# A sequence layer and an expert layer in one kernel: the same 1728 pieces issued in another written order, each PSUM tile in a written bank

## The chip, the cores and the metric

One core of one Trainium2 chip runs the whole kernel. The metric is the device time of one execution in microseconds. The kernel before has three timed runs (504.03, 503.99 and 502.99 us, median 503.99 us) and one profiled execution, from which all rows below come.

## The reference, cut to what matters

The input `u` has 2048 rows of 512 channels. Two layers follow each other, each behind a layer norm, each added to its input:

```python
# layer 1: a long convolution along the rows, one kernel for each channel
P = exp((A * dt)[:, :, None] * pos)            # 512 channels x 128 states x 2048 positions, complex
K = 2 * einsum("dn,dnl->dl", C, P).real        # the convolution kernel of each channel
h = u + irfft(rfft(ln(u), 4096) * rfft(K, 4096))[:2048] + ln(u) * D_skip

# layer 2: 32 heads pick one of 256 experts for each row
q  = einsum("nd,dhc->nhc", ln(h), w_q)         # 512 -> 32 heads x 256
s1 = q[..., :128] @ k1.T ; s2 = q[..., 128:] @ k2.T      # 16 + 16 scores a head
e  = 16 * argmax(s1) + argmax(s2)              # one expert a head and row
h2 = h + sum_over_heads( gelu(ln(h) . u[e]) * v[e] )
```

With one expert a head the softmax over the picked scores is one, so it leaves no work.

## The kernel before, in words

The kernel is one long list of **pieces**. A piece is a small Python function that emits the instructions of one step on one engine (one group of matmuls, one copy, one product, one load), and `Plan.add` registers it with its engine, an estimated cost, the pieces it depends on and the PSUM bank pool that it takes from or gives back to. There are 1728 pieces. `Plan.run` emits them in the order of a written tuple of numbers, `ORDER` (L34 to L115). Each engine executes its own instructions strictly in the order of emission, and semaphores that follow from the data make an engine wait for another. So the tuple alone sets what stands behind what on every engine, the DMA queue of SP included.

The stages, in the order in which they mostly run:

- **Weights `w`.** 32 pieces load parts of `w_q` (L822, 512 KB each on SP), multiply them on PE with the expert keys (`wps`, L828), copy on ACT (L832), turn on PE (L836), copy (L840) and store to DRAM (L844). The result is `w_q` folded with the keys. These pieces wait for nothing but their load and a buffer, and are strewn between all the others.
- **Norm of the input.** SP loads `x` in eight parts of 512 KB, DVE takes statistics (`st`, L232), PE sums them over the partitions (`mu`, L242, and `va`, L255), ACT and DVE make the mean and the reciprocal spread (`pc`, L262 and L264).
- **Tables.** For each of 32 tables GpSimd (POOL in the profile) makes phases (`pg`, L557) and magnitudes (`mg`, L588, and the tail L594), ACT the sine and cosine into PSUM (`t`, L644 to L647), DVE their products (`gf` and `mg`, L651 to L664). PE then folds a table into the convolution kernel (`kps`, L690, 64 matmuls); this last is called the fold below. `pg`, `mg` and `gf` have two buffers, so the magnitudes of table i+2 are not written before the fold of table i has read its own.
- **Transforms.** For four chunks of channels the normed input (`xs`: subtract the mean L505, multiply L508; first transform `s1u`, L471; copied by ACT to `yu`, L474; second `s2yu`, L488, into `U`) and the convolution kernel (`s1k`, `s2yk`) are transformed and multiplied (L732 to L743), and transformed back in two steps, the first into `T` (`ia`, L764, copied at L772 and L777, stored to DRAM at L789), the second in the next layer.
- **The expert layer**, for eight blocks of 256 rows: second inverse transform and sum with the input (`ib` L1036, `h` L1043), the norm (`mean` L1093, `hc` L1073, squares on POOL into `vs`, L1060 to L1062, `hhi`/`hlo` L1076 and L1080), the scores (`sc` L1150), the inner products with all experts (`xu` L1157), the picked expert (`mx`, `eq`, `kq`, POOL's `ks` L1192, `ei` L1199, `ix` L1202) and the weighted sum: turn the index (`ixt` L1242), copy it to all partitions (`bc` L1258, copied by ACT to `idxb` L1262), one-hot rows on DVE (`oh` L1280), count on PE (`cnt` L1290), turn the activations (`ta` L1227), multiply (`actT` L1299), split in a high and a low half (`whi` L1302, `wlo` L1305), the sum over experts (`o` L1324 and L1327), the sum with `h` (`ob` L1332) and the store. The last block does the weighted sum in two halves of 128 rows.

PSUM holds three pools: `psA` with 7 banks up to the end of the transforms (the eighth bank is `pc`), then `psC` with 2 tiles of two banks for the scores and `psD` with 4 banks. In the kernel before each pool has `bufs` equal to its bank count and one tag for all its tiles, so the framework hands out the banks in rotation: the next tile gets the bank of the tile that was taken 7 (or 4) before it, and its first instruction waits until that tile has been read, whether another bank is free or not.

Of the kernel before, what the change touches and what calls it, by code (L numbers as in the profile page):

```python
# [9 lines left out]
F32 = mybir.dt.float32  # L10
# [9 lines left out]
P = 128  # L20
# [7 lines left out]
def view(t, off, dims):  # L28
# [89 lines left out]
class Plan:  # L118
# [5 lines left out]
    def __init__(self, slots):  # L124
        self.group = None
        self.ops, self.wr, self.rd, self.users, self.prev = [], {}, {}, {}, {}
        self.slots = {k: [0.0] * n for k, n in slots.items()}

    def ring(self, name, prev):

        self.prev[name] = prev
# [1317 lines left out]
```

## Time and profile before

| | |
|---|---|
| median of three runs | 503.99 us (502.99 to 504.03) |
| profiled execution, span from first to last instruction | 503.2 us |
| mean share of the span: PE, DVE, POOL, ACT | 89%, 81%, 65%, 59% |
| PE waits in total | 54.2 us, 35.6 of them before 71 us, 5.7 after 490 us |

The profile is of one execution, its span is the time from its first to its last instruction, and it lies 0.8 us under the median of the runs (inside their spread of 1.0 us). PE is TensorE's matmuls, PEld its weight loads, DVE VectorE, ACT ScalarE, POOL GpSimd, SP SyncE, which here only starts DMAs. In a row of a timeline stand the start and the length in us, the engine, the line, the operation, the tile written, `<-`, the tiles read, and in brackets the idle time of the engine before it with what ended it.

### The profile page before, as it was taken

Reading aid. Unit: us, or ns where it says so; the run is one execution under the profiler, and the core shown is the slowest. Engines: PE = TensorE matmul, PEld = TensorE weight load, DVE = VectorE, ACT = ScalarE, POOL = GpSimd, SP = SyncE. Lnnn points to the kernel's source line nnn. Section 1 sums busy time; section 2 is a strip of 40 time slices with the busy share of each in tenths; the row PEclk is TensorE's granted clock in tenths of the full one; section 3 lists DMA queues with packets and bytes.
Section 4 is the critical chain, followed back from the end, with each engine's and each line's share of the span. In section 5 each row is a group of like instructions: output and inputs, shape, how many; then the busy total and the mean of one; then the engine's idle time right before and its main releaser. Section 6 shows DMA issues by size and latency. Waiting matters only on the chain.

```text
span 503.2 us, 16702 instructions
## 1 busy us (share of the span) xinstructions
PE 449.0 (89%) x7206; PEld 390.3 (78%) x7206; DVE 407.8 (81%) x708; ACT 298.3 (59%) x594; POOL 325.5 (65%) x344
## 2 busy tenths in 40 slices
PE   0266879999998999999998889999999999999985
PEld 0144568888997999889997787877878888787874
DVE  5998998899968998899745574888979686978984
ACT  4867799967987588967965362644043430416230
POOL 4989989999999999997824303572163516536130
PEclk9998799999999999999999899999999999999999
DMA  8959474234033300631017689310171311010012
GB/s 253 403 198 381 143 288 148 66 86 179 2 111 124 85 3 1 212 126 45 1 61 259 200 275 283 127 61 1 57 227 55 109 63 43 1 44 0 1 68 62
DMA packets 27362, 61.05 MB, mean 121 GB/s; under 512 B 7028, under 2 KB 14456, under 8 KB 26136
## 3 DMA queue, kind: packets, MB, share of 16 engines
q1 hardware_dynamic: 27136, 59.85, 34.9%
q8 instruction: 57, 0.93, 0.7%
q10 hardware_dynamic: 152, 0.13, 0.1%
q14 instruction: 17, 0.14, 0.1%
HBM read 46.08 MB, written 13.89 MB: 119 GB/s over the span
## 4 chain that ended last, share of the span: by engine, by line
PE 50%; DVE 22%; ACT 10%; POOL 10%; issue 4%; DMA 3%; SPq 1%; ACTq 0%; DVEq 0%; POOLq 0%
PE sc L1150 12%; PE ia L764 9%; DVE oh L1280 5%; PE s2yk L488 3%; PE xu L1157 3%; PE kps L690 3%; PE s2yu L488 3%; POOL pg L557 3%; PE s1u L471 3%; DVE st L232 2%; PE o L1327 2%; PE ib L1036 2%; PE cnt L1290 2%; ACT t L645 2%; POOL mg L594 2%
## 5 line engine op out<-in xcount | busy, mean ns | idle before, releaser
L557 POOL TENSOR_TENSOR pg<-PS 128x1024 int32<-128x1024 int32 x32 | 68.8, 2150 | 0.5
L588 POOL TENSOR_TENSOR mg<-TS 128x1024 f32<-128x1024 f32 x32 | 62.6, 1958 | 7.2 <-PE kps L690 4.5
L1280 DVE TENSOR_SCALAR oh<-idxb,ec_s 128x2048 bf16<-128x2048 bf16 (+1 forms) x72 | 50.3, 757 | 6.8 <-ACT idxb L1262 6.8
L764 PE MATMUL ia<-ca_s,U 128*128 128x128 f32 x256 | 50.6, 280 | 0.4 <-POOL U L743 0.4
L1060 POOL TENSOR_TENSOR vs<-hc 128x256 f32<-128x256 f32 x8 | 7.0, 872 | 62.6 <-ACT hc L1083 62.6
L1192 POOL TENSOR_TENSOR ks<-kq 128x512 f32<-128x512 bf16 x16 | 17.2, 1078 | 45.9 <-DVE kq L1186 44.8
L645 ACT ACTIVATE t<-t,halfpi 128x512 f32<-128x512 f32 x64 | 42.4, 662 | 2.1
L1150 PE MATMUL sc<-w_hi,hhi 128*128 128x480 f32 x128 | 42.4, 412 | 0.0
L644 ACT ACTIVATE t<-pg 128x512 f32<-128x512 int32 x64 | 38.9, 609 | 3.2 <-DVE gf L652 2.2
L764 PEld LDWEIGHTS ia<-ca_s,U 128*128 128x128 f32 x256 | 39.8, 196 | 0.6 <-POOL U L743 0.6
L647 ACT ACTIVATE t<-pg 128x512 f32<-128x512 int32 x64 | 38.2, 608 | 2.8 <-POOL pg L557 1.5
L764 PE MATMUL ia<-ca_s,yk 128*128 128x128 f32 x192 | 38.1, 280 | 0.4 <-DVE mg L664 0.4
L1150 PE MATMUL sc<-w_lo,hhi 128*128 128x480 f32 x128 | 38.4, 380 | 0.0
L1150 PE MATMUL sc<-w_hi,hlo 128*128 128x480 f32 x128 | 38.3, 380 | 0.0
L594 POOL TENSOR_TENSOR mg<-TS 128x512 f32<-128x512 f32 x32 | 37.4, 1170 | 0.4
L690 PE MATMUL kps<-mg 128*32 128x64 f32 x1024 | 34.0, 230 | 3.8 <-DVE mg L664 2.2
L488 PE MATMUL s2yk<-yk,c_s 128*128 128x128 f32 x256 | 34.7, 282 | 1.1 <-ACT yk L474 0.7
L471 PE MATMUL s1u<-c_s,xs 128*64 128x128 f32 x512 | 33.3, 277 | 2.5 <-DVE xs L508 1.6
L690 PE MATMUL kps<-gf 128*32 128x64 f32 x1024 | 33.7, 229 | 1.8 <-issue 1.8
L488 PEld LDWEIGHTS s2yk<-yk,c_s 128*128 128x128 f32 x256 | 30.6, 191 | 4.2 <-issue 1.4
L488 PE MATMUL s2yu<-yu,c_s 128*128 128x128 f32 x256 | 32.6, 279 | 0.3
L471 PEld LDWEIGHTS s1u<-c_s,xs 128*64 128x64 f32 x512 | 27.6, 137 | 5.4 <-DVE xs L508 1.7
(198 smaller groups left out, 1377.5 us busy)
## 6 DMA issues: line engine op xcount, KB each, us to landing
wq<-wq SPq DMA_DIRECT2D x25, 512.0 KB, 4.5
t_d<-T SPq DMA_DIRECT2D x24, 256.0 KB, 3.4
Tb<-t_d SPq DMA_DIRECT2D x8, 768.0 KB, 6.0
x<-xa SPq DMA_DIRECT2D x8, 512.0 KB, 5.6
xs<-xb SPq DMA_DIRECT2D x16, 256.0 KB, 5.3
xt<-xt SPq DMA_DIRECT2D x8, 512.0 KB, 4.8
out<-ob SPq DMA_DIRECT2D x7, 512.0 KB, 3.0
c_s<-wq SPq DMA_DIRECT2D x4, 512.0 KB, 8.3
```

What stands on the lines that cost most here:

```text
L471: T.matmul(ps[64 * k:64 * k + 64, g, :], lhs8(4 * n + g), c1_s[:, k], start=True, stop=True)
L488: T.matmul(ps[:, k, :], c2_s[:, kk, :], y[:, :, kk, :], start=True, stop=True)
L557: G.tensor_tensor(view(pg, 0, [[32, 2 * NC], [8, 4], [1, 8]]), view(t["PS"], 1024 + off, [[1, 2 * NC], [128, 4], [0, 8]]), view(t["PS"], 8 ...
L588: G.tensor_tensor(view(mg, 0, [[96, NC], [8, 8], [1, 8]]), view(ts, 512 + 8 * o, [[8, NC], [1, 8], [0, 8]]), view(ts, 8 * o, [[8, NC], [0, ...
L594: G.tensor_tensor(view(mg, 64, [[96, NC], [8, 4], [1, 8]]), view(ts, 1536 + o, [[1, NC], [64, 4], [0, 8]]), view(ts, 1024 + 8 * o, [[8, NC ...
L644: A.activation(p, pg[:, :, k], AF.Abs)
L645: A.activation(p, p, AF.Sin, scale=-SINSCALE, bias=halfpi)
L647: A.activation(p, pg[:, :, k], AF.Sin, scale=SINSCALE)
L690: T.matmul(kps[32 * q:32 * q + 32, 2 * g + h, :], m[:, d, 64:96], m[:, d, 0:64], start=(e == 0), stop=(e == 1))
L764: T.matmul(ps[:, g, :], t[:, 4 * n + g].rearrange("p a b -> p (a b)"), ca_s[:, s, :], start=(s == 0), stop=(s == 1))
L1150: T.matmul(ps[:, 512 * h:512 * h + 480], t[x_][:, q, ts], I[w_][:, q, 480 * h:480 * h + 480], start=(q == 0 and x_ == w_), stop=(q == 3 an ...
L1280: V.tensor_scalar(oh[:, :, 0:ln], t["idxb"][:, :, sl], S["ec"][:, 4 * e + j:4 * e + j + 1], None, op0=ALU.is_equal)
```

## The change

The change adds and removes no arithmetic. All 1728 pieces, their functions, costs and dependences stay, and so does the number of matmuls. Two things differ.

First, `ORDER` is another order of the same numbers. Second, a dictionary `SLOT` with one digit for every tile that a pool hands out (351 for `psA`, 16 for `psC`, 131 for `psD`) now names the bank. `Plan.run` reads the next digit ahead of each piece that takes a bank, and the tile is made with a tag of its own for each bank, in pools of `bufs=1`. The tile then waits for the tile that had this bank last, 1 to 33 tiles before it in `psA` and 1 to 10 in `psD`, and no longer always 7 or 4. The lines of the changed kernel lie 11 further down (L690 becomes L701).

```diff
 ORDER = (
-    16, 0, 2, 1, 17, 18, 4, 23, 80, 3, 5, 9, 7, 24, 65, 19, 26, 20, 180, 21, 22, 10, 34, 6, 183, 35, 36, 197, 29, 185,
...
+    17, 0, 2, 5, 16, 1, 4, 18, 23, 3, 65, 75, 91, 6, 19, 20, 24, 26, 22, 27, 21, 28, 25, 29, 34, 35, 80, 66, 36, 37,
...
+SLOT = {
+    "psC": "0110101010101010",
...
+}
@@ Plan.__init__
         self.slots = {k: [0.0] * n for k, n in slots.items()}
+        self.slot, self.picks = None, {k: iter(v) for k, v in SLOT.items()}
@@ Plan.run
             done.add(n)
+            for k in self.ops[n][5]:
+                self.slot = next(self.picks[k])
             self.ops[n][3]()
@@ the pools
-    psA = ab.enter_context(tc.tile_pool(name="psA", bufs=7, space=PSUM))
+    psA = ab.enter_context(tc.tile_pool(name="psA", bufs=1, space=PSUM))
-        I["psC"] = ctx.enter_context(tc.tile_pool(name="psC", bufs=2, space=PSUM, reuse_waits="tile"))
-        I["psD"] = ctx.enter_context(tc.tile_pool(name="psD", bufs=4, space=PSUM, reuse_waits="tile"))
+        I["psC"] = ctx.enter_context(tc.tile_pool(name="psC", bufs=1, space=PSUM, reuse_waits="tile"))
+        I["psD"] = ctx.enter_context(tc.tile_pool(name="psD", bufs=1, space=PSUM, reuse_waits="tile"))
@@ one of the places where a tile is made; the others are changed alike
-            d["m"] = psA.tile([P, 4, 128], F32, tag="s", name="mu")[:, 0, 0:64]
+            d["m"] = psA.tile([P, 4, 128], F32, tag=f"s{plan.slot}", name="mu")[:, 0, 0:64]
```

Three places show what the new tuple moves.

On DVE, at the end of the head, where the input's norm becomes known: `xs` are the four normed chunks (the first number is the chunk), `pc` holds the mean and the spread, `gf` and `mg` belong to a table. Before, the steps of chunk 2 and a table's products stand between the steps of chunk 0:

```order
L505 TENSOR_TENSOR xs_2_280<-xs_2_280,pc 128x512
L655 TENSOR_TENSOR gf_905<-mg_888,t_5_871 128x16x32
L264 RECIPROCAL pc<-pc 128x64
L505 TENSOR_TENSOR xs_0_629<-xs_0_629,pc 128x512
L508 TENSOR_TENSOR xs_0_629<-xs_0_629,pc 128x512
L651 SCALAR_TENSOR_TENSOR gf_905<-mg_888,t_5_863 128x16x32
L652 TENSOR_TENSOR gf_905<-mg_888,t_5_863 128x16x32
L508 TENSOR_TENSOR xs_2_280<-xs_2_280,pc 128x512
```

Now:

```order
L516 TENSOR_TENSOR xs_0_921<-xs_0_921,pc 128x512
L275 RECIPROCAL pc<-pc 128x64
L519 TENSOR_TENSOR xs_0_921<-xs_0_921,pc 128x512
L516 TENSOR_TENSOR xs_2_841<-xs_2_841,pc 128x512
L519 TENSOR_TENSOR xs_2_841<-xs_2_841,pc 128x512
L666 TENSOR_TENSOR gf_924<-mg_873,t_5_880 128x16x32
```

Chunk 0 is finished right behind the reciprocal and chunk 2 right behind it, and the table's products come after both. In the same stage SP's list is changed: the last two of the eight loads of `x` stood behind a store of `w_d` and ahead of three loads of `w_q`; now they stand behind two loads of `w_q` and that store. On PE the statistics' sum `mu` stood behind the first two `s1k` pieces and ahead of the next two; now all four, and one `wps` group, stand ahead of it.

On PE, between the folds of tables 16 and 17 (the first and the second half of `kps2_0`). Before, three `s1k` pieces of 8 matmul rows each stand between them:

```order
L690 MATMUL kps2_0_2287<-gf16_2202 32x64 x4
L471 MATMUL s1k1_2_0_2325<-c1_s_84,k1_2_2030 64x128 x8
L471 MATMUL s1k1_3_1_2341<-c1_s_84,k1_3_2255 64x128 x8
L471 MATMUL s1k1_3_0_2353<-c1_s_84,k1_3_2255 64x128 x8
L690 MATMUL kps2_0_2287<-mg17_2218 32x64 x4
```

Now:

```order
L701 MATMUL kps2_0_2315<-gf16_2243 32x64 x4
L499 MATMUL s2yk1_0_2348<-yk1_2098,c2_s_85 128x128 x4
L499 MATMUL s2yk1_2_2362<-yk1_2098,c2_s_85 128x128 x4
L482 MATMUL s1u2_2_0_2367<-c1_s_84,xs2_2_1788 64x128 x8
L482 MATMUL s1u2_3_0_2376<-c1_s_84,xs2_3_2281 64x128 x8
L482 MATMUL s1u2_1_1_2385<-c1_s_84,xs2_1_1574 64x128 x8
L499 MATMUL s2yk1_4_2401<-yk1_2098,c2_s_85 128x128 x4
L482 MATMUL s1u2_1_0_2410<-c1_s_84,xs2_1_1574 64x128 x8
L701 MATMUL kps2_0_2315<-mg17_2239 32x64 x4
```

Seven pieces stand between the folds in place of three: the three `s1k` have gone ahead of the fold of table 16, and three `s2yk` and four `s1u` have come in.

On PE, in the last block's second half, the turned index (`ixt_128`), its copies (`bc`) and the inner products (`xu_1`). Before, twelve matmuls of `xu_1` stand ahead of the first copy:

```order
L1242 MATMUL ixt_128_7078<-ident_b,ix_7060 32x128
L1157 MATMUL xu_1_7083<-u_hi,hhi_6640 128x256
...
L1157 MATMUL xu_1_7083<-u_hi,hlo_6642 128x256
L1258 LDWEIGHTS sel_s
L1258 MATMUL bc_0_128_7097<-ixT_6991,sel_s 128x128
```

Now:

```order
L1253 MATMUL ixt_128_7073<-ident_b,ix_7071 32x128
L1238 MATMUL ta_0_7076<-ident,act_7037 128x128 x2
L1269 LDWEIGHTS sel_s
L1269 MATMUL bc_0_128_7081<-ixT_6992,sel_s 128x128
...
L1269 MATMUL bc_4_128_7086<-ixT_6992,sel_s 128x128
...
L1168 MATMUL xu_1_7130<-u_hi,hhi_6630 128x256
```

Both groups of copies now stand ahead of `xu_1`, and the counts `cnt` of the first half stand between. On DVE the one-hot rows of the second half now precede the multiplication `actT` of the first half, which stood ahead of them.

More of the change, by code (lines that the diff above doesn't have):

```diff
@@ L216 @@
     al, cra, sgn = (pb[:, k] for k in range(3))
-    sg, r64, w0, dt, r = (psA.tile([P, 512], F32, tag="s", name=f"par{k}") for k in range(5))
+    sg, r64, w0, dt, r = (psA.tile([P, 512], F32, tag=f"s{k}", name=f"par{k}") for k in range(5))
     w2 = pb[:, 3]
@@ L252, in var @@
         def var():
-            d["v"] = psA.tile([P, 4, 128], F32, tag="s", name="va")[:, 0, 0:64]
+            d["v"] = psA.tile([P, 4, 128], F32, tag=f"s{plan.slot}", name="va")[:, 0, 0:64]
             for e in range(2):
@@ L456, in bank @@
     def bank(job, nm, at="ps"):
-        job[at] = psA.tile([P, 4, 128], F32, tag="s", name=nm)
+        job[at] = psA.tile([P, 4, 128], F32, tag=f"s{plan.slot}", name=nm)
         return job[at]
@@ L1030, in mm @@
                 if 0 in js:
-                    job["ps"] = I["psD"].tile([P, 4, 128], F32, tag="m", name=f"ib{b}_{a}")
+                    job["ps"] = I["psD"].tile([P, 4, 128], F32, tag=f"m{plan.slot}", name=f"ib{b}_{a}")
                 for j in js:
@@ L1103, in mm @@
         def mm():
-            job["ps"] = I["psD"].tile([P, 256], F32, tag="m", name=f"mean{b}")
+            job["ps"] = I["psD"].tile([P, 256], F32, tag=f"m{plan.slot}", name=f"mean{b}")
             T.matmul(job["ps"], S["ones"], t["hs"], start=True, stop=True)
@@ L1121, in mm @@
         def mm():
-            ps = job["ps"] = I["psD"].tile([P, 2], F32, tag="m", name=f"var{b}")
+            ps = job["ps"] = I["psD"].tile([P, 2], F32, tag=f"m{plan.slot}", name=f"var{b}")
             for k in range(2):
@@ L1145, in mm @@
             if q == 0:
-                job["ps"] = I["psC"].tile([P, 1024], F32, tag="s", name="sc" + nm)
+                job["ps"] = I["psC"].tile([P, 1024], F32, tag=f"c{plan.slot}", name="sc" + nm)
             ps = job["ps"]
@@ L1153, in mx_ @@
         def mx_():
-            ps = jx["ps"] = I["psD"].tile([P, 256], F32, tag="m", name="xu" + nm)
+            ps = jx["ps"] = I["psD"].tile([P, 256], F32, tag=f"m{plan.slot}", name="xu" + nm)
             for q in range(4):
@@ L1224, in mm @@
             def mm(k=k, job=job):
-                tp = job["ps"] = I["psD"].tile([P, 2, 128], F32, tag="m", name=f"ta{b}_{k}")
+                tp = job["ps"] = I["psD"].tile([P, 2, 128], F32, tag=f"m{plan.slot}", name=f"ta{b}_{k}")
                 for e in range(2):
@@ L1239, in mm @@
             def mm(job=job, ks_=ks_, lo=lo):
-                job["ps"] = tp = I["psD"].tile([32, 256], BF16, tag="m", name=f"ixt{b}_{lo}")
+                job["ps"] = tp = I["psD"].tile([32, 256], BF16, tag=f"m{plan.slot}", name=f"ixt{b}_{lo}")
                 for k in ks_:
@@ L1286, in mm @@
                     if e == 0:
-                        job["ps"] = I["psD"].tile([P, 2, 256], F32, tag="m", name=f"cnt{b}_{lo}")
+                        job["ps"] = I["psD"].tile([P, 2, 256], F32, tag=f"m{plan.slot}", name=f"cnt{b}_{lo}")
                     for hg in range(8):
```

8 lines of the change are left out of this document (5 added, 3 removed), and 161 rows, old and new, of the table ORDER.

## The prediction, made before the changed kernel was run

> **What bounds the kernel now.** I read the page first, for who is busy when. The second fence row is the busy time of each engine, the two below it are the busy share of PE and of POOL in 40 slices of 12.6 us, in tenths:
>
> ```profile
> span 503.2 us, 16702 instructions
> ...
> PE 449.0 (89%) x7206; PEld 390.3 (78%) x7206; DVE 407.8 (81%) x708; ACT 298.3 (59%) x594; POOL 325.5 (65%) x344
> ...
> PE   0266879999998999999998889999999999999985
> ...
> POOL 4989989999999999997824303572163516536130
> ```
>
> PE is at 9 nearly everywhere behind the sixth slice. So I cut the span at the places where that digit falls and asked for the busy time of each engine in each stretch (length, then PE, PE's weight loads, DVE, ACT, POOL, each with its count, then granted clock, DMA share and GB/s):
>
> ```profile
> 0.00:71.00 71.00, 35.40 (x700) 25.39 (x702) 61.62 (x169) 51.38 (x133) 60.25 (x71) 0.93 0.80 287
> 71.00:260.00 189.00, 184.94 (x3528) 170.55 (x3526) 163.97 (x269) 154.09 (x297) 172.90 (x157) 1.00 0.25 82
> 260.00:305.00 45.00, 39.83 (x640) 36.59 (x640) 26.42 (x46) 23.18 (x49) 10.11 (x8) 0.96 0.73 235
> 305.00:440.00 135.00, 133.73 (x1643) 111.41 (x1631) 106.96 (x146) 49.66 (x81) 63.82 (x84) 1.00 0.27 91
> 440.00:490.00 50.00, 47.53 (x554) 40.27 (x554) 43.51 (x69) 18.15 (x34) 18.41 (x26) 1.00 0.06 24
> 490.00:503.20 13.20, 7.53 (x170) 6.12 (x167) 5.30 (x12) 1.83 (x4) 0.00 (x0) 1.00 0.25 77
> ```
>
> PE's idle time is 35.6 us in the head, 4.1 in the tables, 5.2 around the third chunk's inverse, 1.3 and 2.5 in the expert layer and 5.7 in the tail. The change leaves every matmul in place, so it can win only from these 54 us, and only 13 of them lie in the 419 us between 71 and 490. In the tables POOL is nearly as full as PE (172.9 of 189 us against 184.9), so an order that asks POOL to wait can lose as quickly as it wins.
>
> **Part 1, the head.** From here the timeline of single engines carries the sum. On PE and DVE, and one load of `x` and one weight group from the chain of waits:
>
> ```profile
> 42.29 5.55 DMA x<-xa
> ```
>
> ```profile
> 47.87 0.87 DVE L232 BATCH_NORM_STATS2 st<-x 128x6 f32<-128x128 f32 x4 [1.34 <-DMA x<-xa]
> ```
>
> ```profile
> 39.14 0.87 PE wps L828 x16
> ```
>
> ```profile
> 59.39 0.68 PE L242 MATMUL mu<-st,eq 128*128 128x64 f32 x4 [0.39 <-DVE st L232]
> 67.92 1.97 PE L471 MATMUL s1u<-c_s,xs 128*64 128x128 f32 x32 [1.58 <-DVE xs L508]
> 70.77 2.11 PE L471 MATMUL s1u<-c_s,xs 128*64 128x128 f32 x32 [0.88 <-ACT yu L474]
> ```
>
> The head ends when `xs` is there: PE waits 1.58 us for chunk 0 and 0.88 before chunk 2. By the new order two more `s1k` pieces and one weight group stand ahead of `mu`, 0.87 us the group. Walking that order with the durations of this trace, `mu` comes about 2 us later, but behind the norm DVE now finishes chunk 0 and then chunk 2 without a table's products between, so that `s1u` starts about 0.8 us later than 67.92. Against that stand the group already done (0.87) and the second wait, which goes (0.88): 0.8 - 0.87 - 0.88 = **-1.0 us**. Both ends: all 2.46 us of waits go, or the later `mu` costs its 2 us in full, -2.5 to +2.0. I take the walk's value since every row in it was seen. That the 0.88 is put down to a copy which empties a PSUM bank fits the fixed rotation; the named banks can only help there.
>
> **Part 2, the folds of tables 16 and 17.** PE's timeline has its two longest waits of the tables here, rows of the same view:
>
> ```profile
> 150.50 0.32 PE L690 MATMUL kps<-mg 128*32 128x64 f32 x8 [0.56 <-DVE gf L652]
> ...
> 151.53 2.84 PE L471 MATMUL s1k<-c_s,k 128*64 128x128 f32 x48
> ...
> 156.88 0.26 PE L690 MATMUL kps<-gf 128*32 128x64 f32 x4 [1.78 <-issue]
> ```
>
> The first, 0.56 us, is for the table's last product. Three `s1k` pieces now stand ahead of this fold, 2.84 us by the second row, so the table is there: -0.56. The second is no wait for data: it falls inside a fold and the profile finds no releaser ("issue"). In that window the page of DMA, its share of the 16 engines in 40 slices and the row of one of its queues on the whole page, show
>
> ```profile
> DMA  9378799976369899969988999762020000000000
> ```
>
> ```profile
> q8 instruction: 57, 0.93, 0.7%
> ```
>
> engines at 9 tenths up to about 155 us and a queue that brings instructions, 0.93 MB in 57 packets or 16 KB each. I read the stall as a packet of instructions that came late behind the stores of `T`. PE executes a fold's 64 matmuls and 64 weight loads in 1.0 us (150.50 to 151.53), far denser than the 48 in the next 2.84 us; between the two folds there now stand seven pieces of about 0.95 us (2.84 / 3), 6.6 us in place of 2.84, so the packet has 3.8 us more. The stores still lie there, so I count two thirds: -1.2 of 1.78, between 0 and all of it. Together **-1.8 us** (-2.3 to 0).
>
> The Trainium skill ("Runtime: NRT & Kernel Launch", section "Instruction fetch mechanics") says that instructions come in blocks of 16 KiB over a queue of the sequencer's own and that crossing a block is mostly hidden. The packet size agrees; the 1.78 us row does not look hidden. By the page the stall would be something else, this part would be worth 0.56 us, and the whole about 1.2 us less.
>
> **Part 3, from the last fold to the expert layer.** On PE, then DVE's first and last product in the same stretch, then the chain's row before the expert layer:
>
> ```profile
> 272.66 0.43 PE L828 MATMUL wps<-wq,ka_s 128*32 128x128 f32 x8 [1.32 <-DMA wq<-wq]
> ...
> 281.84 0.71 PE L764 MATMUL ia<-ca_s,U 128*128 128x128 f32 x2 [0.36 <-POOL U L743]
> ```
>
> ```profile
> 269.31 0.69 DVE L732 TENSOR_TENSOR yu<-s2yk,U 128x512 f32<-128x512 f32 x1 [5.28 <-ACT ki L739]
> ...
> 280.48 0.68 DVE L733 TENSOR_TENSOR U<-s2yk,U 64x512 f32<-64x512 f32 x1
> ```
>
> ```profile
> 299.51 2.23 DVE w_lo L925 x2
> ```
>
> The wait of 1.32 us for a weight load goes, since the last loads of `w_q` now leave before the last stores of `T`. It is worth nearly nothing: DVE makes its sixteen products from 269.31 to 281.16 nearly without pause and POOL's last `U` releases `ia`, so PE would only wait later. I count -0.3. One conversion `w_lo` fewer stands ahead of the first `h` on DVE, half of 2.23 us; I count half of that, -0.5, since PE has other work there. Together **-0.8 us** (-2.4 to +0.5, the last for a weight group that would now stand ahead of a fold).
>
> **Part 4, the tail.** PE, then DVE, in the last block's second half:
>
> ```profile
> 488.18 0.39 PE L1157 MATMUL xu<-u_hi,hhi 128*128 128x256 f32 x1
> ...
> 489.82 0.39 PE L1258 MATMUL bc<-ixT,sel_s 32*128 32x128 bf16 x4
> ```
>
> ```profile
> 492.13 0.42 DVE L1299 TENSOR_TENSOR actT<-cnt,actT 128x256 f32<-128x256 f32 x1 [2.37 <-PE ta L1227]
> 492.47 3.25 DVE L1280 TENSOR_SCALAR oh<-idxb,ec_s 128x1024 bf16<-128x1024 bf16 x8
> ...
> 499.06 0.69 DVE L1332 TENSOR_TENSOR ob<-o,h 128x512 f32<-128x512 f32 x1 [1.55 <-PE o L1324]
> ```
>
> The copies `bc` wait 1.64 us (488.18 to 489.82) behind `xu`; now they are ahead of it, and four of the eight one-hot rows, 4 x 0.41 = 1.62 us, fit into DVE's idle 2.37 us. The path behind DVE then shortens by 1.62 at most; but `xu`, whose result the second half also needs, now comes later by `bc` and 64 counts, and I take **-1.0 us** (-1.6 to +0.5).
>
> **What else moves.** All other waits of PE between 71 and 260 us are 4.06 - 0.56 - 1.78 = 1.7 us; a rewritten order will have such places of its own, whose positions I can't walk to a tenth. I take as many again: **+1.7 us** (0 to 4).
>
> The sum is -1.0 - 1.8 - 0.8 - 1.0 + 1.7 = -2.9 us, against a span of 503.2. The median of the runs is 504.0, 0.8 above this execution's span; with the same 0.8 the forecast is 503.2 - 2.9 + 0.8 = **501.1 us**. A change of 0.2%, 1.0 us, is about what a measurement of this kernel can tell from none.
>
> **The rivals.**
>
> *No change.* PE is busy for 406 of the 419 us from 71 to 490, and what one place wins the next one waits for. For it: the 1.32 us of part 3. Against it: parts 1 and 4 lie outside that stretch. Half of the sum goes, or more: 503 to 505 us, chance 0.13.
>
> *Slower, by the two buffers of the magnitudes.* The end of the fold of table 24 on PE, then POOL:
>
> ```profile
> 208.68 0.29 PE L690 MATMUL kps<-gf 128*32 128x64 f32 x8
> ```
>
> ```profile
> 212.26 1.96 POOL L588 TENSOR_TENSOR mg<-TS 128x1024 f32<-128x1024 f32 x1
> ...
> 234.28 1.96 POOL L588 TENSOR_TENSOR mg<-TS 128x1024 f32<-128x1024 f32 x1 [2.78 <-PE kps L690]
> ...
> 240.78 1.95 POOL L588 TENSOR_TENSOR mg<-TS 128x1024 f32<-128x1024 f32 x1 [1.31 <-PE kps L690]
> ...
> 252.16 1.95 POOL L588 TENSOR_TENSOR mg<-TS 128x1024 f32<-128x1024 f32 x1 [1.05 <-issue]
> ```
>
> The first of these may not start before the fold of table 24 has ended, which was at 208.97, 3.3 us earlier. In the new order four `s1u`, three `s1k`, three `s2yk` pieces and a weight group more stand ahead of that fold: by rows above some 0.95 us for each of ten (2.84 / 3) and 0.87, in all 10.4 us. POOL would then wait 10.4 - 3.3 = 7.1 us; its later idle time gives back 2.78 + 1.31 + 1.05 = 5.1, so table 31 is 2.0 us late. The fold of table 26 has three `s2yu` pieces and two weight groups more ahead of it, 4.6 us, with no slack in the trace (234.28 is where it ended); if that adds in full it is 6.6. The middle, 4.3 us, gives 505.4 us. It decides where PE has not run some 4 us ahead by fold 24; parts 1 and 2, if they come, give 2.8 of these. Against it: PE's work between the folds of 24 and 31 is smaller by what was moved ahead. Chance 0.14.
>
> *Slower, by the head.* SP's last two loads of `x` now stand behind two loads of `w_q`, which wait for a buffer. Three such loads took SP
>
> ```profile
> 45.50 7.37 SPq L822 DMA_DIRECT2D wq<-wq  x3
> ```
>
> so two can put the issue off by 4.9 us. In the trace 11.5 us lie between the landing (42.29 + 5.55 = 47.84) and `mu`, filled with statistics and products on DVE; if those all queue behind the later load, `mu` is 4.9 us late, PE has 0.87 us to do meanwhile, and 501.1 + 1.0 + 4.0 gives 506.1 us. Chance 0.11.
>
> *The one-hot rows beside POOL.* DVE, one such row while POOL works and one while it doesn't, and what POOL does at the time:
>
> ```profile
> 465.00 1.22 DVE L1280 TENSOR_SCALAR oh<-idxb,ec_s 128x2048 bf16<-128x2048 bf16 x1
> ```
>
> ```profile
> 466.80 0.74 DVE L1280 TENSOR_SCALAR oh<-idxb,ec_s 128x2048 bf16<-128x2048 bf16 x1
> ```
>
> ```profile
> 464.60 1.06 POOL L1062 TENSOR_TENSOR vs<-vs,hc 128x256 f32<-128x256 f32 x1
> ```
>
> A row takes 0.48 us longer beside POOL. The new order puts three rows of the last block but one right behind the step after which POOL sums `ks`: 3 x 0.48 = 1.4 us on DVE, in place of the 1.0 us won in the tail: 501.1 + 2.4 = 503.5 us, chance 0.05. The Trainium skill ("SBUF — State Buffer", section "Who interferes with whom") has this as a rule: VectorE and GpSimd share a pair of ports under an exclusive lock. The rows agree in direction.
>
> **How the numbers follow.** The forecast's own case, 498 to 502.9 us, has chance 0.57. No change and the one-hot rows end within 1.0 us of 504.0: 0.18. The two slower rivals make 0.25. The range reaches down to 496.5, where the allowance of 1.7 isn't needed and the head and part 3 come at their ends (501.1 - 1.7 - 1.5 - 1.6 = 496.3), and up to 506.5, which holds the prices of both slower rivals. Half of what these cost may come on top, and that is the tenth or two left out.
>
> **What would show it.** Right: `s1u` starting within a microsecond of 68 us without a second wait; folds 16 and 17 with no wait over 0.5 us; `ia` of the last chunk as late behind the last fold as before; `bc` ahead of `xu` and DVE's idle 2.37 us gone. Wrong: POOL's magnitudes waiting for folds by more than 5 us in the tables (the second rival), statistics waiting for `x` past 52 us (the third), or waits of PE in places that none of the parts names that add up to more than 4 us.

## The result and the profile after

The changed kernel takes 523.3 us (median of four runs, 521.3 to 524.2) against 503.5 us of the kernel before in the same comparison: **1.037 times as long, 95% interval 1.033 to 1.042, slower by 18 to 21 us**. The forecast was 501.1 us, faster, with a range up to 506.5.

The page of the profiled execution, the rows that answer to those shown of before, and the granted clock of PE:

```profile
span 521.8 us, 16705 instructions
...
PE 459.5 (88%) x7206; PEld 396.1 (76%) x7206; DVE 419.7 (80%) x708; ACT 303.9 (58%) x598; POOL 333.6 (64%) x344
...
PE   0356899999999999999997949998999899998986
...
POOL 4699898999999999978915002654355244635240
PEclk9997779999999999999997997999999999999999
```

The same number of matmuls, and 10.5 us more of PE's busy time, 11.9 more of DVE's and 8.1 more of POOL's. No arithmetic was added, so instructions got longer or were interrupted. For PE a part of this is the granted clock, 0.966 in the mean against 0.986. The same stretches as in the prediction, the last one up to the new end:

```profile
0.00:71.00 71.00, 36.21 (x669) 26.07 (x673) 58.71 (x164) 50.96 (x128) 57.95 (x72) 0.87 0.72 249
71.00:260.00 189.00, 186.86 (x3568) 172.73 (x3562) 164.96 (x271) 157.30 (x304) 175.24 (x156) 0.99 0.32 105
260.00:305.00 45.00, 38.19 (x565) 35.42 (x561) 25.60 (x46) 22.70 (x48) 10.12 (x8) 0.92 0.58 185
305.00:440.00 135.00, 126.14 (x1551) 102.74 (x1555) 104.28 (x132) 46.02 (x71) 60.08 (x73) 0.97 0.28 89
440.00:490.00 50.00, 47.24 (x545) 37.63 (x535) 41.68 (x56) 20.48 (x37) 23.76 (x28) 1.00 0.09 31
490.00:521.80 31.80, 24.87 (x342) 21.54 (x341) 24.45 (x42) 6.48 (x13) 6.45 (x8) 0.98 0.15 51
```

Up to 260 us PE does as much as before (669 + 3568 matmuls against 700 + 3528). From 305 to 440 us it is busy 126.1 us where it was 133.7. Since fixed stretches hold different work once a kernel is late, I read four landmarks off PE's timeline in both traces: the end of the last `ia`, the start of the first `sc`, the end of the last `sc`, the end of the span.

| stage | before, us | after, us | difference |
|---|---|---|---|
| first layer, up to the last `ia` | 297.8 | 299.8 | +2.0 |
| handover, last `ia` to first `sc` | 9.2 | 13.4 | +4.2 |
| score stage, first to last `sc` | 170.8 | 184.8 | +14.1 |
| tail, behind the last `sc` | 25.4 | 23.7 | -1.7 |

So the first layer, on which most of the prediction's working went, moved by 2 us; the loss is in the expert layer. The last two rows belong together: 134 matmuls `o` ran ahead of the last `sc` before and 144 do now, so some 3 us of PE's work (37.5 us busy before, 40.7 after) have only crossed the landmark. Stage and tail together grew by 12.4 us.

In the handover it is PE's waits that grew. `ib`, from the last `ia` to the first `sc`, before and after (instructions, busy us and mean ns, then the idle time before them and what ended it):

```profile
L1036 PE MATMUL ib<-cb,Tb 128*32 128x64 f32 x192 | 5.0, 221 | 0.9 <-issue 0.9
L1036 PE MATMUL ib<-cb,T 128*32 128x64 f32 x64 | 4.5, 221 | 1.2 <-ACT T L777 0.6 <-DVE T L777 0.6
```

```profile
L1047 PE MATMUL ib<-cb,Tb 128*32 128x64 f32 x192 | 4.5, 223 | 7.1 <-issue 5.2 <-ACT w_hi L935 1.9
```

These are 7.1 us in place of 2.1, and 5.2 of them end without a releaser in the profile ("issue"). What happened on SP and then PE:

```profile
293.92 3.18 SPq L1025 DMA_DIRECT2D xt<-xt  x2
297.15 7.18 SPq L1017 DMA_DIRECT2D Tb<-t_d  x2
```

```profile
312.91 0.33 PE L1047 MATMUL ib<-cb,Tb 128*32 128x64 f32 x3 [3.95 <-issue]
```

The load of `Tb` for block 1 stands behind two loads of `xt`, which wait until 293.92; before, it had been issued at 288.31, ahead of them. Two `Tb` loads of 768 KB, another `xt` and a `cb` therefore fall into the time of the first `ib`. PE stands still for 3.95 us in the middle of a group of them (at the 249th of the 256 matmuls of blocks 0 and 1), and before that for 1.24 us at the 137th; a `Tb` lands 6.5 to 6.9 us behind its issue, that of block 1 at about 304. The trace's packets on the queue that brings 16 KB of instructions at a time point to what it waited for. In each of the two traces, and in two of the experiments below, the matmul behind a long wait of `kps` or `ib` starts 1.3 to 1.5 us after the end of one packet:

| | PE's wait, us | the packet, us | from its end to PE's next |
|---|---|---|---|
| before, `kps` | 155.10 to 156.88 | 154.58 to 155.54 | 1.34 |
| before, `ib` | 306.02 to 306.78 | 304.04 to 305.43 | 1.35 |
| after, `kps` | 206.40 to 207.42 | 205.08 to 206.06 | 1.36 |
| after, `ib` | 303.83 to 305.07 | 302.86 to 303.81 | 1.26 |
| after, `ib` | 308.96 to 312.91 | 310.54 to 311.64 | 1.27 |
| order alone, `ib` | 307.48 to 309.75 | 307.27 to 308.29 | 1.46 |
| old first layer, new expert layer, `ib` | 310.68 to 313.56 | 311.09 to 312.30 | 1.26 |

I read this as PE having run out of instructions: `ib` are short matmuls (64 columns), and the packet came late behind the loads. No view shows the instructions that PE holds; but a trace has 57 such packets, one in about 9 us, and seven waits that all end within 0.2 us of the same distance from one are hardly chance. (A wait of 1.2 us of `wps` in the head of the kernel before, at 46.63, does not fit: it ends 1.7 us behind a packet.) In the window from 304 to 313 us the DMA engines' shares, in 40 slices, stand at 7 to 9 from 305 to about 310.3, and the packet starts at 310.54:

```profile
DMA  0000088799999997989797999998552212010009
```

In the stretches behind the wait the granted clock is lower too (the number before the DMA share):

```profile
310.00:316.00 6.00, 3.09 (x15) 2.50 (x16) 3.47 (x5) 2.49 (x4) 3.64 (x5) 0.70 0.53 158
316.00:322.00 6.00, 6.00 (x52) 4.76 (x50) 0.00 (x0) 0.00 (x0) 1.05 (x2) 0.73 0.28 107
```

That is 12 us at about 0.7, an estimated 3 us of PE at full clock, and since it lies mostly behind the first `sc`, it stands in the score stage's row. In two experiments below the clock also fell soon after the long wait of `ib`: to 0.51 from 311.0 to 314.4 us (order alone) and to 0.50 from 315.0 to 318.4 us (old first layer, new expert layer).

Of the score stage, first the kernel before, then the changed one, in the columns of the stretches above:

```profile
307.00:477.80 170.80, 169.26 (x1988) 141.02 (x1983) 137.17 (x191) 62.12 (x103) 77.85 (x103) 1.00 0.21 72
```

```profile
313.30:498.10 184.80, 177.20 (x1996) 143.66 (x1992) 149.24 (x190) 63.08 (x103) 86.03 (x104) 0.98 0.19 63
```

DVE's busy time (the third pair) grew by 12.1 us over the same number of instructions, while the rest of the stage, in which DVE is idle, hardly moved: 33.6 us before, 35.6 after. PE, the fuller engine, now waits for it. Its longest waits in the stage (total, times, longest), before and after:

```profile
PE cnt L1290 <- DVE oh L1280: 1.0, 2, 0.6
```

```profile
PE ixt L1253 <- DVE ix L1213: 3.2, 5, 1.2
PE cnt L1301 <- DVE oh L1291: 2.7, 4, 0.9
```

With smaller ones PE's waits grew from 1.5 to 7.2 us. These 5.7 us, the 3 us of moved `o` and the 3 us of clock make up most of the 14.1; the other 2 or so are not placed. Which of DVE's instructions grew shows the grouping by line (busy us, then mean ns), before and after:

```profile
L1280 DVE TENSOR_SCALAR oh<-idxb,ec_s 128x2048 bf16<-128x2048 bf16 x56 | 42.9, 824 | 6.8 <-ACT idxb L1262 6.8
L1080 DVE TENSOR_TENSOR hlo<-hc,hhi 128x1024 fp32r<-128x1024 f32 x7 | 8.7, 1238 | 3.5 <-ACT hhi L1076 3.4
...
L1202 DVE SCALAR_TENSOR_TENSOR ix<-ei 128x32 bf16<-128x32 int32 x16 | 6.1, 381 | 0.6
L1305 DVE TENSOR_TENSOR wlo<-actT,whi 128x512 fp32r<-128x512 f32 x7 | 5.6, 801 | 0.9 <-ACT whi L1302 0.9
L1199 DVE TENSOR_SCALAR ei<-ks 128x64 int32<-128x64 int32 x16 | 4.6, 289 | 2.1 <-POOL ks L1194 2.1
```

```profile
L1291 DVE TENSOR_SCALAR oh<-idxb,ec_s 128x2048 bf16<-128x2048 bf16 x56 | 46.8, 888 | 0.5 <-ACT idxb L1273 0.5
L1091 DVE TENSOR_TENSOR hlo<-hc,hhi 128x1024 fp32r<-128x1024 f32 x7 | 10.0, 1433 | 0.9 <-ACT hhi L1087 0.9
L1213 DVE SCALAR_TENSOR_TENSOR ix<-ei 128x32 bf16<-128x32 int32 x16 | 8.3, 520 | 0.6
...
L1210 DVE TENSOR_SCALAR ei<-ks 128x64 int32<-128x64 int32 x16 | 7.0, 439 | 4.7 <-POOL ks L1205 4.7
L1316 DVE TENSOR_TENSOR wlo<-actT,whi 128x512 fp32r<-128x512 f32 x7 | 7.0, 1003 | 1.3 <-ACT whi L1313 1.2
```

These five kinds alone, all of which read SBUF only, took 3.9 + 1.3 + 2.2 + 2.4 + 1.4 = 11.2 us more. One place shows what they met, POOL and DVE in the changed kernel:

```profile
364.46 1.05 POOL L1203 TENSOR_TENSOR ks<-kq 128x512 f32<-128x512 bf16 x1 [6.58 <-DVE kq L1197]
365.59 2.61 POOL L1205 TENSOR_TENSOR ks<-ks 128x256 f32<-128x256 f32 x3
```

```profile
364.50 1.55 DVE L1316 TENSOR_TENSOR wlo<-actT,whi 128x512 fp32r<-128x512 f32 x1
365.98 3.42 DVE L1291 TENSOR_SCALAR oh<-idxb,ec_s 128x2048 bf16<-128x2048 bf16 x4
```

As soon as DVE has made `kq`, POOL starts its sum `ks`, and the new order has put a split `wlo` (1.55 us here, 0.80 in the mean before) and one-hot rows right behind `kq` on DVE. Overlaying the two timelines, the share of a DVE instruction's time in which POOL worked too went from 29% to 49% for `oh`, 16 to 61 for `hlo`, 36 to 58 for `wlo`, 42 to 71 for `ei`, 64 to 78 for `ix`; and fell for those that read PSUM and kept their durations (`mx` 49 to 32, `ob` 50 to 23). One-hot rows without POOL beside them take the same in both traces (0.745 us in the mean before, 38 of the 56 long ones; 0.742 after, 25 of them); `hlo` takes 1.2 us without POOL and 1.7 beside it all along. The order shows it without a trace: of the three pieces that follow each of the 16 `kq` on DVE, 12 were one-hot rows or splits before, 24 are now.

### The profile page after: what moved, and what is told of

Same layout as the page of the kernel before. It is cut to its first block, busy times and chain, and to the rows that moved or that the text cites. A ratio compares the mean times of both kernels' runs of the same rounds, so it can differ in the third digit from the quotient of the medians.

```text
span 521.8 us, 16705 instructions
## 1 busy us (share of the span) xinstructions
PE 459.5 (88%) x7206; PEld 396.1 (76%) x7206; DVE 419.7 (80%) x708; ACT 303.9 (58%) x598; POOL 333.6 (64%) x344
## 5 line engine op out<-in xcount | busy, mean ns | idle before, releaser
L599 POOL TENSOR_TENSOR mg<-TS 128x1024 f32<-128x1024 f32 x32 | 62.5, 1955 | 11.2 <-PE kps L701 7.8
L1291 DVE TENSOR_SCALAR oh<-idxb,ec_s 128x2048 bf16<-128x2048 bf16 (+1 forms) x72 | 54.2, 806 | 0.5 <-ACT idxb L1273 0.5
L1203 POOL TENSOR_TENSOR ks<-kq 128x512 f32<-128x512 bf16 x16 | 19.2, 1202 | 48.9 <-DVE kq L1197 43.4
L701 PE MATMUL kps<-mg 128*32 128x64 f32 x1024 | 35.2, 236 | 2.5 <-DVE mg L675 2.1
L1205 POOL TENSOR_TENSOR ks<-ks 128x256 f32<-128x256 f32 (+2 forms) x48 | 33.6, 699 | 3.8
L701 PE MATMUL kps<-gf 128*32 128x64 f32 x1024 | 34.9, 234 | 1.0 <-issue 1.0
```

Of the source, the lines that this page charges most:

```text
L599: G.tensor_tensor(view(mg, 0, [[96, NC], [8, 8], [1, 8]]), view(ts, 512 + 8 * o, [[8, NC], [1, 8], [0, 8]]), view(ts, 8 * o, [[8, NC], [0, ...
L701: T.matmul(kps[32 * q:32 * q + 32, 2 * g + h, :], m[:, d, 64:96], m[:, d, 0:64], start=(e == 0), stop=(e == 1))
L1205: G.tensor_tensor(kt_[:, :, 0:w], kt_[:, :, 0:w], kt_[:, :, w:2 * w], op=ALU.add)
L1291: V.tensor_scalar(oh[:, :, 0:ln], t["idxb"][:, :, sl], S["ec"][:, 4 * e + j:4 * e + j + 1], None, op0=ALU.is_equal)
```

## The theories and the experiments

**Theory O**: the order costs, in the expert layer. **Theory B**: the written banks cost. Under O, **C**: the order sets DVE's SBUF work beside POOL's sums; **D**: the expert layer's order makes results late wherever POOL is. C splits again in **T**, the traffic costs, and **L**, the sum `ks` only comes later. All ratios are to the kernel before on the same chip.

**Order alone.** The pools as before, only the tuple:

```diff
-    16, 0, 2, 1, 17, 18, 4, 23, 80, 3, 5, 9, 7, 24, 65, 19, 26, 20, 180, 21, 22, 10, 34, 6, 183, 35, 36, 197, 29, 185,
+    17, 0, 2, 5, 16, 1, 4, 18, 23, 3, 65, 75, 91, 6, 19, 20, 24, 26, 22, 27, 21, 28, 25, 29, 34, 35, 80, 66, 36, 37,
...
```

> The new order of pieces, with the pools of the kernel before (the framework picks the banks). Theory O, the order alone costs the time: 521 to 525 us, as the changed kernel. Theory B, the banks written down make instructions wait for each other: 502 to 506 us. If both have a part, a time between.

Measured 522.3 us, ratio 1.035 (1.028 to 1.041), in the band of theory O. The banks of the changed kernel make no difference that these runs can tell; the order carries the loss.

**Banks alone.** The tuple of before, in the code of after, with other digits:

```diff
 SLOT = {
-    "psC": "0110101010101010",
+    # one digit for each tile in the old order: the bank of after where free, else the one free longest
...
```

> The old order of pieces, with banks written down: of the 498 tiles 364 have the bank that the changed kernel gives them, the others the free bank given back longest ago. Theory O: 503 to 505 us, no change. Theory B: 510 us or more.

Measured 554.9 us, ratio 1.100 (1.094 to 1.105). This stretch of its profile shows where, against 184.9 us of PE before and 186.9 after:

```profile
71.00:260.00 189.00, 155.22 (x2970) 140.70 (x2967) 141.40 (x230) 131.06 (x248) 155.05 (x146) 0.98 0.27 91
```

In the tables a bank that is free in the list is still being read when its turn comes: one `wps` group waited 3.6 us for DVE's `gf`, of which it reads nothing. So banks chosen badly can cost 50 us. The time lies in the band of theory B, but 134 of the 498 digits are not those of the changed kernel, and with its own digits the run above saw no cost. Theory B is out for this change, and my choice of digits, not the writing down, is what this run measures.

**Which half of the order.** Two tuples spliced at piece 1104, where the expert layer begins, with the pools as before:

```python
x = iter(n for n in EXPERT_ORDER if n >= 1104)
ORDER = [n if n < 1104 else next(x) for n in FIRST_LAYER_ORDER]
```

> New order for the first 1104 pieces (weights, tables, transforms), old order for the 624 pieces of the expert layer, its loads included; the framework picks the banks. Theory O with the loss in the expert layer's own order: 503 to 507 us, since the changed kernel is only 2.0 us late at its last ia matmul. If instead the handover from the first layer carries the delay: 510 us or more.

> Old order for the first 1104 pieces, new order for the 624 of the expert layer; the framework picks the banks. Theory O with the loss in the expert layer's own order: 518 to 523 us. If the loss comes from the first layer or from the banks: 503 to 506 us.

New first layer with the old expert layer: 507.8 us, ratio 1.006 (1.003 to 1.008), some 3 us slower. Old first layer with the new expert layer: 524.4 us, ratio 1.039 (1.033 to 1.046), the whole loss. The two medians lie 0.8 and 1.4 us above the bands of theory O, far from the others. The first run also speaks against the granted clock as the cause: its profiled execution had a mean of 0.971, near the 0.966 of the changed kernel, and took 508.1 us.

**The handover.** The new order, but SP's pieces of the expert layer in the old one, and the reverse:

```diff
 # SP's pieces of the expert layer, in the tuple (cut to the place of block 1; others differ too)
-    ... xt1, xt0, Tb1 ...
+    ... Tb1, xt0, xt1 ...
```

> New order everywhere except SP, whose loads and stores of the expert layer stand as before (the transformed rows of block 1 ahead of the two loads of xt); the framework picks the banks. If the handover costs by that load: 3 to 6 us faster than the new order alone, and no wait of 3 us of ib for Tb. If not: no change.

> Old order everywhere, only SP's loads and stores of the expert layer in the new order (two loads of xt ahead of the transformed rows of block 1). If the handover's loss lies in that: 507 to 510 us, with waits of ib for Tb of 3 us or more. If it needs the other engines' new order as well: 503 to 505 us.

The first took 517.2 us, ratio 1.025 (1.018 to 1.033), and its handover 7.5 us (11.0 with the order alone), without a wait of `ib` that has no releaser. SP's rows:

```profile
287.45 0.58 SPq L1007 DMA_DIRECT2D Tb<-t_d  x1
293.39 3.18 SPq L1015 DMA_DIRECT2D xt<-xt  x2
```

The second took 508.6 us, ratio 1.008 (1.005 to 1.011), with a handover of 11.6 us in place of 9.2, but no wait of 3 us of `ib`; its longest there, 2.0 us, is for ACT's copy of `T`, and the granted clock is 0.50 for 3.4 us behind it. The load order costs in both, 2.4 us alone and 3.5 in the new order; the long wait needs the other engines' order as well. The expectations spoke of a wait for `Tb`; where the wait was longest it was, by the reading above, for the instructions behind it on the same DMA engines, and a wait for `Tb` itself, 1.9 us, shows only with the old first layer and the new expert layer. The intervals of the first run and of the order alone overlap, so the times by themselves don't settle the 5 us between them. The handover does settle that the loads cost there: it is 11.0 to 14.2 us in all six traces with the new loads, 7.5 to 10.0 in all eleven with the old ones.

**GpSimd's sums.** `ks` cut to one short addition, in the old and the new order:

```diff
-            G.tensor_tensor(kt_, d["kq"][:, :, 0:8], d["kq"][:, :, 7:15], op=ALU.add)
-            for w in (4, 2, 1):
-                G.tensor_tensor(kt_[:, :, 0:w], kt_[:, :, 0:w], kt_[:, :, w:2 * w], op=ALU.add)
+            G.tensor_tensor(kt_[:, :, 0:1], d["kq"][:, :, 0:1], d["kq"][:, :, 7:8], op=ALU.add)
```

> The kernel before, with GpSimd's sum ks cut to one short addition in place of four (the rest of the sum is left out). Theory C, the new order puts DVE's one-hot rows, index steps and splits beside GpSimd's sums, where they take longer: here few of them stand beside it, 0 to 5 us faster than before. Theory D, results of DVE come late in the new order wherever GpSimd is: both orders gain alike.

> The changed kernel with the same cut of ks. Theory C: 8 to 14 us faster than the changed kernel, more than the kernel before gains by the cut, and DVE's busy time in the expert layer back by some 10 us. Theory D: the gap of 17 to 20 us between the two orders stays.

502.1 us (ratio 0.994, 0.991 to 0.997) and 515.0 us (1.018, 1.012 to 1.025). The cut is worth 0.6% of the time in the old order and 1.9% in the new, as C has it, though a gap of 12.9 us stays, which still holds the handover and the first layer.

> The changed kernel, with three memsets of the ks tile and one short addition in place of the four additions (the sum is left out), so that GpSimd's result comes as late as before but GpSimd reads nothing meanwhile. Theory C, if reading beside DVE is what costs: 6 to 12 us faster than the changed kernel, near the short ks. Theory L, the lateness of ks and not its traffic: no faster than 2 us.

518.5 us, ratio 1.026 (1.020 to 1.033). This run tells nothing apart: the memsets wait for no input, so they ran before `kq` was there, and `ks` was neither as late nor the traffic at the same place.

To take out the handover too, the old loads, and POOL's sums over the four parts (`vs` and `hs`) cut from three additions to one beside the cut of `ks`:

```diff
             G.tensor_tensor(s_, q[:, 0], q[:, 1], op=ALU.add)
-            G.tensor_tensor(s_, s_, q[:, 2], op=ALU.add)
-            G.tensor_tensor(s_, s_, q[:, 3], op=ALU.add)
```

> The kernel before, with GpSimd's sum ks cut to one short addition and its sums vs and hs over the four parts cut from three additions to one (the rest of both sums is left out). Theory C, GpSimd beside DVE: DVE's busy time near its least, 498 to 502 us. It is the yardstick for the next run.

> New order with the old order of the expert layer's loads, and the same cuts of GpSimd's sums (the rest of both sums is left out). Theory C: within 1 to 4 us of the kernel before with the same cuts, since handover and GpSimd are then taken out and only the 1 to 2 us of the first layer are left. Theory D, the order of the expert layer's other pieces loses by itself: 8 us or more above it.

499.6 us (0.989, 0.985 to 0.994) and 506.2 us (1.002, 1.000 to 1.005): 6.5 us apart, between the two expectations. In the two profiled executions 3.2 us of it are the first layer and 3.5 the score stage and the tail together. The score stage of the new order with old loads, then of these two (old order, new order):

```profile
306.80:490.50 183.70, 176.09 (x2000) 142.28 (x1992) 151.82 (x194) 66.11 (x107) 87.25 (x105) 0.99 0.21 69
```

```profile
305.00:473.40 168.40, 168.37 (x1986) 140.99 (x1983) 129.81 (x192) 62.56 (x104) 18.04 (x30) 1.00 0.22 74
```

```profile
308.30:482.10 173.80, 171.85 (x1999) 141.30 (x2000) 134.07 (x196) 65.51 (x107) 20.18 (x30) 1.00 0.21 71
```

With POOL's sums the new order's stage is 183.7 - 170.8 = 12.9 us longer and DVE's busy time 14.6; with the sums cut, 5.4 and 4.3. So about 7.5 of the 12.9 us hang on POOL's sums, and the waits say the same: in the new order with old loads PE waits 6.7 us for `ix`, `oh` and `hs`, with the sums cut not at all. Of the other 5.4 us, some 3 are the ten matmuls `o` that the new order puts ahead of the last `sc` (144 against 134 here as well); the tail gives back 1.9 of them (23.8 us, then 21.9). PE's other waits make 1.8 us against none.

**Traffic or lateness.** In the new order with old loads, first `ks` early and the four additions into a spare tile behind it, then `ks` late with writes in place of additions:

```diff
+            G.tensor_tensor(kt_[:, :, 0:1], d["kq"][:, :, 0:1], d["kq"][:, :, 7:8], op=ALU.add)
+            kd = I["hp"].tile([P, 64, 8], F32, tag="kd", name=f"kd{n}", bufs=1)
-            G.tensor_tensor(kt_, d["kq"][:, :, 0:8], d["kq"][:, :, 7:15], op=ALU.add)
+            G.tensor_tensor(kd, d["kq"][:, :, 0:8], d["kq"][:, :, 7:15], op=ALU.add)
             for w in (4, 2, 1):
-                G.tensor_tensor(kt_[:, :, 0:w], kt_[:, :, 0:w], kt_[:, :, w:2 * w], op=ALU.add)
+                G.tensor_tensor(kd[:, :, 0:w], kd[:, :, 0:w], kd[:, :, w:2 * w], op=ALU.add)
```

> New order with old loads (517 us). GpSimd first makes ks by one short addition (the sum is left out), then does the same four additions into a spare tile that nobody reads: its traffic stays, its lateness goes. Theory T, traffic beside DVE costs: 514 us or more and DVE's busy time in the expert layer as high as before the cut. Theory L, ks comes late: 508 to 512 us.

> New order with old loads. GpSimd waits for kq with a short addition, then writes a spare tile four times by memset, then makes ks by a short addition (the sum is left out): ks as late as in the full sum, but almost nothing is read meanwhile. Theory T, if reading is what costs DVE: 508 to 512 us. Theory L: 514 us or more.

516.4 us (1.024, 1.020 to 1.028) and 520.2 us (1.031, 1.027 to 1.036). The score stage of the first:

```profile
309.10:492.00 182.90, 174.60 (x2000) 141.63 (x1992) 149.90 (x193) 66.03 (x107) 93.97 (x120) 1.00 0.21 69
```

With `ks` early and the traffic kept, the stage is 0.8 us shorter than with the full sum, at a granted clock of 1.00 for 0.99, and DVE nearly as busy: the lateness of `ks` is not what the cut took away. What is left is the traffic, or the time that POOL is busy with it while its next sums wait; these runs keep both or take both away. The second run refutes the simple form of T: its stage has 185.6 us with 148.2 of DVE, so writes beside DVE did not free it, and DVE waited more. Its instructions divide: the splits went back to 1.25 us (`hlo`) and 0.75 (`wlo`) in the mean, near their 1.25 and 0.72 with the sums cut, but the one-hot rows, 0.91 us against 0.89 with the additions, did not. That a `ks` that is later still costs time isn't shown: the stage is 1.9 us longer than with the full sum, but the granted clock in it was 0.98 in place of 0.99, which is as much.

**Moving DVE's work away from POOL.** New order with old loads; nine pieces that read PSUM go ahead of rows and splits behind `kq`, as here for `kq` of `sc1` and the split `hlo` of block 2:

```diff
 # DVE, behind kq of sc1
-    hlo2, mx, eq
+    mx, eq, hlo2
```

> New order with the old order of the loads, and on DVE nine pieces that read PSUM (maxima, comparisons, sums with the transform) put ahead of the one-hot rows and splits that stood right behind a weighing kq, where GpSimd starts its sum. Theory C: 1 to 4 us faster than the new order with old loads. If the moved pieces come too early for their inputs: no gain or slower.

519.1 us, ratio 1.029 (1.025 to 1.033): no faster, and its stage says why.

```profile
307.20:492.30 185.10, 175.72 (x1996) 141.46 (x1992) 144.38 (x193) 66.02 (x107) 81.46 (x105) 1.00 0.21 68
```

DVE's busy time did fall, from 151.8 to 144.4 us, by these nine moves. But its other time grew from 31.9 to 40.7: pieces that stand earlier wait for their inputs and hold the rest up (`ob` waits 7.3 us for PE's `o` in place of 2.1, and PE waits 3.8 us for the later `hlo`, where it had not). So this run doesn't show that a less busy DVE makes the stage shorter; that rests on the cut sums. Taking the contention away by a local swap buys nothing; the old order had both, work for the time of the sums and inputs that were there.

**The tail alone.** The first 1656 pieces old, the last 72 in the new order:

```python
ORDER = OLD[:1656] + [n for n in NEW if n not in set(OLD[:1656])]
```

> The first 1656 pieces in the old order, the last 72 in the new one (the tail of the last block). By the prediction's part 4: 0.5 to 1.6 us faster than before. If the tail is set by the products behind the late xu: no change.

505.2 us, ratio 1.002 (0.999 to 1.004). In the profile the tail is 2.0 us shorter (23.4 against 25.4), but the score stage is 1.4 longer (172.2), since here too 144 of the matmuls `o` stand ahead of the last `sc`; together they are 0.5 us shorter. The first layer, whose order is that of before, ended 2.1 us later in this execution. The interval reaches from 0.5 us faster to 2.1 slower, so the expected gain of 0.5 to 1.6 us isn't there; no version that does all the work beats the kernel before.

## Why the prediction was wrong, point by point

- **What bounds the kernel.** This is the step that failed. I took the 1.3 us of PE's idle time from 305 to 440 us as all that an order could move there, and put the expert layer between handover and tail at nothing in the sum. But a stretch where PE is full can still get longer. DVE was busy 79% of it, and that time is no constant; the order changed it by 12 us in the score stage, and PE, with 1.5 us of waits there before, now waits 7.2. The last of the signs of being wrong came true by this: waits of PE that no part names, 5.2 us of `ib` and most of these 7.2.
- **The rival with the one-hot rows** had the right mechanism with the wrong place and price. "The new order puts three rows of the last block but one right behind the step" looked only at the tail, 1.4 us, chance 0.05. The same step stands 16 times in the expert layer, and splits and index steps pay as well: 12.1 us of DVE time, some 7.5 us of the stage by the cuts. The Trainium skill ("SBUF — State Buffer", section "Who interferes with whom") also says that an instruction with at most one SBUF input outside the 2-port modes does not contend; the maxima over PSUM agree, with a mean of 1.15 us in both traces.
- **Part 3, the handover.** Only the loads of `w_q` were followed on SP, not those of the expert layer behind them. There lay 4.2 us of loss, with 1.24 and 3.95 us of standing still, behind which the granted clock was 0.70 and 0.73 for two stretches of 6 us. What part 2 says of instructions that come late behind transfers was the tool for it, and I did not carry it from the folds to `ib`, though a row of before (0.76 us at 306.02) had the same mark.
- **Part 3, the last chunk.** The weight load's wait of 1.32 us did go, and the work that hid the wait for DVE's products went with it, as the text feared. PE now waits here, 2.3 us in place of 0.4 (the row of 281.84). The rows run at half the later pace (0.43 us for two matmuls, 0.22 later) up to 288.5 now, and did so up to 285.3 before:

```profile
281.48 0.66 PE L775 MATMUL ia<-ca_s,yu 128*128 128x128 f32 x2 [1.58 <-DVE yu L743]
282.82 0.79 PE L775 MATMUL ia<-ca_s,U 128*128 128x128 f32 x2 [0.68 <-POOL U L754]
```

- **Part 1, the head.** Both waits ahead of `s1u` are gone, as said. But `mu` came 4.5 us later and not 2, and `s1u` 3.6 later and not 0.8:

```profile
63.89 0.62 PE L253 MATMUL mu<-st,eq 128*128 128x64 f32 x4
...
71.53 4.63 PE L482 MATMUL s1u<-c_s,xs 128*64 128x128 f32 x64
```

  The rival of the late `x` came near for `mu` (4.9 us; the last loads of `x` were issued 6.9 us later), but its sign didn't show, since no row of `st` waits for `x`, and its price was wrong: PE had other pieces to do. By 71 us it had started 669 matmuls against 700, by 260 us 4237 against 4228.
- **Part 2, the folds.** No wait is left at tables 16 and 17; the two waits of 0.56 and 1.78 us went. A wait of the second kind, inside a fold and without a releaser, stands at table 23 now, so the sum there is -1.3 us where -1.8 was forecast. The reading of it holds: the table of packets above has it. The Trainium skill ("Runtime: NRT & Kernel Launch", section "Instruction fetch mechanics") has the blocks of 16 KiB and calls their crossing mostly hidden; behind busy DMA engines it cost 0.8 to 4.0 us here, if the reading above holds.

```profile
206.11 0.29 PE L701 MATMUL kps<-gf 128*32 128x64 f32 x7
207.42 0.22 PE L701 MATMUL kps<-gf 128*32 128x64 f32 x1 [1.03 <-issue]
```

- **Part 4, the tail**: `bc` stands ahead of `xu` and DVE's idle 2.37 us are gone, as said, and the landmark's tail is 1.7 us shorter. But the run of the tail alone has no such gain as a whole (0.5 us at most), since `o` only moved ahead of the landmark: the forecast of -1.0 is not borne out, and the -1.7 agrees with it by luck.
- **The rival of the two buffers** did not decide: the last fold ended at 264.9 us, 1.7 us later than before, in place of the 4.3 us feared; POOL's magnitudes waited 6.5 us for folds from 71 to 265 us, and 4.5 before.
- **The text on the banks** ahead of the prediction, and part 1 with it, speaks of a fixed rotation. The banks that the kernel before was built with don't rotate: its first six weight tiles lie in banks 2, 1, 3, 5, 0 and 1. Nothing in the sum hung on it but the remark on the 0.88 us.

Shown by runs: the order and not the banks; the expert layer and not the first; the loads in the handover; the share of POOL's sums. Only argued: that the `ib` waits are for instructions, and that POOL's sums act by lengthening DVE's instructions and not by keeping POOL busy; some 2 us of the stage are not placed.

## What to carry to other kernels

When an order is changed, list for the second busiest engine what its instructions will run beside, at every repeat of the loop and not at one place; durations read from the old trace hold only for the old neighbours. A stage in which the first engine is full has little room to win and much to lose. And follow the transfers of the next stage on their own queue past every load that waits for a buffer; where they landed in a dense run of matmuls here, PE stood still up to 3.95 us.

## What the runs showed of the hardware that I had not expected

- Waits of PE without a releaser, up to 3.95 us, in seven places where a dense run of matmuls met busy DMA engines (59% or more in the 3 to 6 us ahead), and PE's next instruction there 1.3 to 1.5 us behind the end of a packet of 16 KB. Not every such run had one: in the new order with old loads, 207 matmuls in 5 us (302 to 307 us) beside DMA engines 67% busy had no wait of this kind.
- DVE's SBUF work can double beside POOL's additions in single instructions (`wlo` 1.55 us against a mean of 0.80), and POOL pays too: its first addition of `ks` took 1.08 us in the mean before and 1.20 after.
- Replacing additions by memsets on POOL did not give DVE its time back (148.2 us busy against 151.8): the splits with two inputs in SBUF got theirs (`hlo` 1.25 us for 1.44 in the mean), the one-hot rows did not (0.91 for 0.89).
- The order of the first layer being the same, the last `ia` ended at 297.8 us in one execution and 299.9 and 299.6 in two others (the new tail, the new expert layer): about 2 us between executions at that place.
